# Two alternating layers on one core: weights, squares and normalized rows in one ring of eight places, with later reloads and later block sums

## The chip, the cores and the metric

The kernel runs on 1 core of a Trainium2 chip. The metric is the device time of one execution in microseconds (us). Five engines work side by side, each through its own instructions in program order: TensorE (PE; its weight loads are listed as PEld), VectorE (DVE), ScalarE (ACT), GpSimd (POOL) and SyncE (SP). An instruction waits on semaphores until what it needs is there, and everything behind it on the same engine waits with it. All DMA transfers of this kernel are issued from SP, so a transfer that has to wait holds up every transfer behind it.

## The reference, cut to what matters

```python
def A(q, k, v, shift_k, ssm_k, ssm_D):         # S = 2048 tokens, D = 1024 channels
    k_shift = ...                              # causal convolution with 4 taps, per channel
    kv = k_shift * v
    y = irfft(rfft(kv_pad) * rfft(ssm_k_pad))  # causal convolution over all S tokens, per channel
    return q * (y + kv * ssm_D)

def B(x, w1, b1, w2, b2):                      # F = 3584
    h = x @ w1 + b1
    r = where(h > 0, h, 0)
    return (r * r) @ w2 + b2

x = A_q
x = x + A(layernorm(x), A_k, A_v, A_shift_k, A_ssm_k, A_ssm_D)
x = x + B(layernorm(x), B_w1, B_b1, B_w2, B_b2)
x = x + A(layernorm(x), A_k, A_v, A_shift_k, A_ssm_k, A_ssm_D)
x = x + B(layernorm(x), B_w1, B_b1, B_w2, B_b2)
```

Everything is fp32. The long convolution `y` doesn't depend on x, so it is computed once and serves both layers.

## The kernel before, in words

**Units.** The work runs over 8 units, `ORDER` (line 35): a unit is one layer and one block of 512 tokens (four tiles of 128), and does matrix layer B for it. Unit 0 is block 0 of layer 0, unit 1 block 0 of layer 1, and so on; unit 7 is the last. Where two units follow each other on the same block (0 to 1, 6 to 7), a passage (`chain`) turns one unit's output straight into the next one's input, in halves of two tiles.

**Steps.** A unit is a list of steps (`steps`, lines 680 to 703). A step uses one weight tile of 128 x 512: for the first product (m1) half of a column block of w1, for the second (m2) a row block and half of w2. As fp32 products, each number is split into a high part and the rest, and three matmuls (`mm3`, lines 270 to 273) make one product; a step has 12 matmuls of 512 columns. PE does them in step order.

**The life of a weight tile.** It is loaded raw from HBM on SP (`w_load`, lines 731 and 734), ACT copies its high part into the pair tile `whl` (`w_hi`, line 742), and DVE, in the passages also POOL, subtracts to get the rest (`w_lo`, line 750). Some tiles are also stored to HBM as a split pair (`w_store`, line 757, `wd_m`), and later uses load the pair, ready split, with one DMA (line 740); `from_pair` says which. Unit 0 uses raw tiles nearly alone; from unit 1 on about 70 of 112 tiles are pairs. `whl` has six places; raw tiles `wr` had four.

**How far ahead.** `w_advance` (line 759) runs once at each step s with its weight w: subtractions up to w + 3 (`W_LO`), copies up to w + 4 (`W_HI`), pair loads up to w + 5 (`W_PAIR`), raw loads up to w + 8 (`W_LOAD`) as long as fewer than `RAWS` = 4 raw tiles wait for their subtraction. A raw load thus takes the place that the subtraction of the same step, or one just before it, has to free. A pair load takes the place of the weight six before it, and is issued when that weight's last step lies before s.

**Squares and rows.** After each m1 block `relu2` (line 1102) makes `r` on ACT (relu, square, high part; lines 1105 to 1108) and one step later DVE subtracts (line 1113); `r` had two places of its own. Normalized rows `xn` (lines 631, 1143, 1182), which PE transposes for the next unit, had two as well.

**The convolution.** It is done by blocks of 256 tokens in a transformed domain, alongside units 0 to 5. `fwd_x` and `fwd_g` transform the inputs (ticks of their own; PE transposes and matmuls in the two banks `pt`, DVE and ACT around them) and store the spectra (xd, gd). `prod_stream` (line 439) loads for a group of channels pairs of tiles cx and cg (lines 510 and 512, two places each), multiplies them into `cp` (`mult`, line 445, three places) and sums over the blocks (`red`, line 449). It has a clock of its own, `lag`, that ticks once per product; the product stands two ticks behind its loads, its sum three, and the closing steps (`fin`: combine, split, back transform, scale, store) from tick four on. One product in 14 (`VMOD`) runs on DVE, the others on POOL. How many products go into a step is paced by `pace`, up to two per step in unit 0.

**Within a step** the order of issue is: delayed work that is due (`lag.tick`), `w_advance` (subtractions, copies and pair loads, raw loads), the matmuls, `w_store`, then the convolution's products and transforms.

**The first block.** Block 0's convolution and the first 8 weight tiles are ordered by a planner with costs (`Plan`, line 87; `weight`, line 1036), which also knows how many places `wr` has.

The functions that the change touches, and what calls them:

Of the kernel before, what the change touches and what calls it, by code (L numbers as in the profile page):

```python
# [33 lines left out]
EPS = 1e-5  # L34
ORDER = [(0, 0), (1, 0), (0, 1), (0, 2), (1, 1), (1, 2), (0, 3), (1, 3)]
PAIRS = ((2, 0), (0, 1), (1, 2))
W_LOAD, W_HI, W_LO, W_PAIR = 8, 4, 3, 5
RAWS = 4
PAIR_GAP = 10
PRO_M = "GGV"  # L40
VMOD = 14
FWD_WAIT = 4
PLAN_H = 0.5
VX = 300
# [141 lines left out]
def tile_h3_mlp(ctx: ExitStack, tc: tile.TileContext, q, kT, vT, shk, ssmT, ssmD, w1, b1, w2, b2,  # L186
# [244 lines left out]
        for g in streams:  # L431
            next(g, None)

    count = [0]
    done = set()

    plag = Later()
# [1 line left out]
    def prod_stream():  # L439
        lag = plag  # L440
        sums, inv = [0, 0], [0, 0]

        def mult(st, xt, gt, j, e):
            pr = cv.tile([P, CU, j + 1], F32, name="cp", bufs=3)
            e.tensor_mul(pr.rearrange("p c i -> p i c"), xt[:, 0:j + 1], gt[:, j::-1])  # L445
            st["pr"] = pr

        def red(st, sm, ty, jj):
# [47 lines left out]
        for sb in range(1, NB):  # L496
            nb = BT * sb + BT
            for ch in range(KT):
                while (sb, ch) not in fwd_done:
                    lag.tick()  # L500
                    yield None
                for g in (2 * ch, 2 * ch + 1):
                    while sums[0] - sums[1] >= 2:
                        lag.tick()
                        yield None
                    sums[0] += 1
                    sm = cv.tile([P, 3, BT, CU], F32, name="sm", bufs=2)
                    for ty, (xi, gi) in enumerate(PAIRS):
                        xt = cv.tile([P, nb, CU], F32, name="cx", bufs=2)
                        SY.dma_start(xt, XD[xi][g, :, :nb])  # L510
                        gt = cv.tile([P, nb, CU], F32, name="cg", bufs=2)
                        SY.dma_start(gt, GD[gi][g, :, :nb])
                        for jj in range(BT):
                            j = BT * sb + jj
                            count[0] += 1
                            e = V if count[0] % VMOD == 0 else G
                            st = {}
                            lag.at(2, mult, st, xt, gt, j, e)
                            lag.at(3, red, st, sm, ty, jj)
                            if ty == 2 and jj == BT - 1:  # L520
                                lag.at(4, fin, st, sm, sb, g, 0)
                            lag.tick()
                            yield (j + 1) * CU * 1e-3
        while lag.due:
# [77 lines left out]
    def prep_b(l, b, lag):  # L602
# [4 lines left out]
        def stage(st, tt, k):  # L607
# [7 lines left out]
            elif k == 1:  # L615
                x = st["x"]
                for h in range(2):
                    sl = slice(h * 512, (h + 1) * 512)
                    yt = st["y"][h]
                    V.scalar_tensor_tensor(yt, x[:, sl], mv[:, tt, 0:1], yt, op0=OP.subtract, op1=OP.mult)  # L620
                    V.scalar_tensor_tensor(x[:, sl], yt, r[:, tt:tt + 1], x[:, sl], op0=OP.mult, op1=OP.add)
            elif k == 2:
                st["mv"] = pre.tile([P, 1, 2], F32, name="mv2", bufs=4)
                stats(st["x"], st["mv"][:, 0])
                st["ve"], st["sd"] = rstd_a(st["mv"])
                SY.dma_start(X1[b][:, tt], st["x"])
            elif k == 3:
                st["r"] = rstd_b(st["ve"], st["sd"])
                st["xn"] = []
                for kh in range(2):  # L630
                    xn = ml.tile([P, 512], F32, name="xn", bufs=2)
                    normalize(xn, st["x"][:, kh * 512:(kh + 1) * 512], st["mv"][:, 0, 0:1], st["r"])
                    st["xn"].append(xn)
            elif k == 4:
                st["o"] = []
                for kh in range(2):
                    o = ps1()
                    for c in range(4):
                        PE.transpose(o[:, c * P:(c + 1) * P], st["xn"][kh][:, c * P:(c + 1) * P], ident)  # L639
                    st["o"].append(o.rearrange("p (k t) -> p k t", k=4))  # L640
            else:
# [78 lines left out]
    def from_pair(w):  # L720
        return split_kept(wsrc[w]) and w - first_w[wsrc[w]] >= PAIR_GAP

    def w_load():
        w = ptr["load"]
        ptr["load"] += 1
        if from_pair(w):
            return
        k, c, a, i = wsrc[w]
        raw = raws[w] = mw.tile([P, 512], F32, name="wr", bufs=RAWS)
        if k == "m1":  # L730
            SY.dma_start(raw, w1[c * FC + a, :, 4 * i:4 * i + 4])
        else:
# [3 lines left out]
    def w_hi():  # L736
        n = ptr["hi"]
        t = his[n] = mw.tile([P, 2, 512], F32R, name="whl", bufs=6)
        if from_pair(n):
            SY.dma_start(t.bitcast(F32), WD[wsrc[n]])  # L740
        else:
            A.copy(t[:, 0], raws[n])  # L742
        ptr["hi"] += 1

    def w_lo():
        n = ptr["lo"]
        t = wts[n] = his.pop(n)
        if not from_pair(n):
            e = WLO.get(phase[0], "V")
            ENG[e[n % len(e)]].tensor_sub(t[:, 1], raws.pop(n), t[:, 0].bitcast(F32))  # L750
        ptr["lo"] += 1

    def w_store(w):
# [2 lines left out]
            WD[key] = dram.tile([P, 2, 512], F32, name="wd_" + "_".join(map(str, key)))  # L756
            SY.dma_start(WD[key], wts[w].bitcast(F32))

    def w_advance(s, w, first=False):
        n = len(wsrc)  # L760

        def free(k):
            return k < n and (k < 6 or last_use[k - 6] < s)

        def ahead(k):
            return w + (W_PAIR if k < n and from_pair(k) else W_HI)
# [2 lines left out]
            w_lo()  # L769
        while free(ptr["hi"]) and ptr["hi"] <= ahead(ptr["hi"]) and ptr["hi"] < ptr["load"]:  # L770
            w_hi()
        while ptr["load"] < n and len(raws) < RAWS and ptr["load"] <= w + W_LOAD:
            w_load()
        while ptr["lo"] <= w:
            if ptr["hi"] <= ptr["lo"]:
                w_hi()
            w_lo()
# [4 lines left out]
    def first_block():  # L782
# [305 lines left out]
            wts.pop(w)  # L1088
        for k in ptr:
            ptr[k] = n  # L1090
        return [x.t for x in xT]

    xT = first_block()
# [7 lines left out]

    def relu2(st, k):
        if k == 0:
            r = st["r"] = ml.tile([P, T], F32, name="r", bufs=2)
            A.activation(r, st["o"], AF.Relu, bias=b1t[:, st["f"]:st["f"] + 1])  # L1105
            A.activation(r, r, AF.Square)  # L1106
            st["hi"] = ml.tile([P, T], F32R, name="rh", bufs=FC + 1)
# [2 lines left out]
                give(st["o"])  # L1110
        else:
            st["lo"] = ml.tile([P, T], F32R, name="rl", bufs=FC + 1)
            V.tensor_sub(st["lo"], st["r"], st["hi"].bitcast(F32))  # L1113

    def evict(os, accs, dh):
        d = slice(dh * 512, (dh + 1) * 512)
# [3 lines left out]
    def chain(accs, b, xh, xl, ready):  # L1120
# [13 lines left out]
        def astep(st, n):  # L1134
# [3 lines left out]
                V.scalar_tensor_tensor(x, y, r, x, op0=OP.mult, op1=OP.add)  # L1138
            else:
                for h in range(2):  # L1140
                    z = ml.tile([P, 512], F32, name="xn", bufs=2)
# [3 lines left out]
                    G.tensor_add(x[:, sl], x[:, sl], y[:, sl])  # L1145

        def evict1(st, os, dh):
            d = slice(dh * 512, (dh + 1) * 512)
# [4 lines left out]
        def stage(st, k):  # L1153
# [23 lines left out]
            elif k in (5, 6):  # L1177
# [1 line left out]
                x, m, r = accs[tts[n]], st["mv"][:, n, 0:1], st["r"][:, n:n + 1]  # L1179
                st["o", n] = []  # L1180
                for kh in range(2):
                    xn = ml.tile([P, 512], F32, name="xn", bufs=2)
# [9 lines left out]
            elif k in (7, 8):  # L1192
                n = k - 7
                for kh in range(2):
                    o = ps1()
                    for c in range(4):
                        PE.transpose(o[:, c * P:(c + 1) * P], st["o", n][kh][:, c * P:(c + 1) * P], ident)
                    st["o", n][kh] = o.rearrange("p (k t) -> p k t", k=4)
            else:
                n = k - 9  # L1200
                for kh in range(2):
# [215 lines left out]
```

## Time and profile before

| | us |
|---|---|
| median of 3 runs | 3097.34 (3093.33 to 3100.3) |
| the profiled execution, its time | 3092.24 |
| its span, first to last instruction | 3090.4 |
| PE busy | 2862.2 (93%) |
| DVE busy | 1713.9 (55%) |
| ACT busy | 979.7 (32%) |
| POOL busy | 882.1 (29%) |
| moved by DMA | 704.73 MB, mean 228 GB/s |

All times in the rows below are counted from the first instruction of the profiled execution. In the view by stretches a row gives the stretch, its length, then for each engine the busy time and the number of instructions, the share of full clock that TensorE was granted, the share of the 16 DMA engines that was busy, and GB/s. In the views of waits a row reads: who waited, on which line, for whom; us in total, times, longest. SPq is the queue of SyncE. In the timeline a row gives start, duration, engine, line, operation, tiles and shapes, and in brackets how long the engine stood idle before it and what ended that. The order in which the program issues its work, with the step at which a tile's place was freed, can be counted from the code without any run; where the text counts so, it says "program order".

### The profile page before, as it was taken

How to read it: one execution, taken by the hardware profiler on the slowest of the kernel's cores; microseconds unless marked ns; L12 is line 12 of the kernel's file. 1: busy time of each engine (PE TensorE's matmuls, PEld its weight loads, DVE VectorE, ACT ScalarE, POOL GpSimd, SP SyncE). 2: the span in 40 equal slices, each digit the busy share in tenths (PEclk: the TensorE clock that was granted, in tenths of full speed). 3: DMA queues.
4: the chain of work that ended last, by engine and by line, in shares of the span. 5: the costliest groups of instructions: out<-in, count | busy, mean ns of one | idle time of the engine just before them, and what ended most of it. 6: DMA issues, size and time to landing. Idle time of an engine off the chain costs nothing.

```text
span 3090.4 us, 37259 instructions
## 1 busy us (share of the span) xinstructions
PE 2862.2 (93%) x13512; PEld 2389.9 (77%) x13512; DVE 1713.9 (55%) x2600; ACT 979.7 (32%) x1741; POOL 882.1 (29%) x639
## 2 busy tenths in 40 slices
PE   6877777777999999999999999999999999989999
PEld 6865665656877888888888888888888888878887
DVE  7875545656576777877676664446422621262122
ACT  3332323232333343234323342224222422223222
POOL 5543223334253415542433243331300100030000
PEclk8878888888999999999999999999999999989999
DMA  6445776666787888978887777668654755464543
GB/s 200 132 169 198 233 262 216 224 220 241 255 293 262 274 301 290 324 264 276 288 298 256 249 269 275 228 227 291 216 167 155 265 162 173 143 219 150 185 145 126
DMA packets 332375, 704.73 MB, mean 228 GB/s; under 512 B 55960, under 2 KB 135968, under 8 KB 332192
## 3 DMA queue, kind: packets, MB, share of 16 engines
q1 hardware_dynamic: 332192, 702.36, 67.2%
q8 instruction: 106, 1.74, 0.2%
q14 instruction: 77, 0.63, 0.1%
HBM read 575.36 MB, written 126.88 MB: 227 GB/s over the span
## 4 chain that ended last, share of the span: by engine, by line
PE 66%; DMA 9%; DVE 7%; POOL 2%; SPq 2%; issue 2%; ACT 1%; POOLq 0%; DVEq 0%; ACTq 0%
PE p L271 21%; PE p L273 21%; PE p L272 21%; DMA cg<-gd 4%; POOL cp L445 1%; DVE whl L750 1%; PE pt L272 1%; PE pt L273 1%; PE pt L271 1%; DMA yt<-yd 1%; DMA xd<-fx 1%; DMA wr<-w 1%; DVE sm L449 1%; PE p L639 1%; DMA wd_m<-whl 0%
## 5 line engine op out<-in xcount | busy, mean ns | idle before, releaser
L445 POOL TENSOR_TENSOR cp<-cx,cg 128x384 f32<-128x384 f32 (+5 forms) x268 | 482.8, 1814 | 1128.7 <-DMA cg<-gd 1043.3
L271 PE MATMUL p<-whl,rh 128*128 128x512 f32 x1792 | 722.3, 403 | 20.8 <-DVE acc L1118 16.3
L272 PE MATMUL p<-whl,rh 128*128 128x512 f32 x1792 | 718.8, 401 | 18.9 <-DVE whl L750 13.3
L273 PE MATMUL p<-xh,whl 128*128 128x512 f32 (+1 forms) x1864 | 715.2, 384 | 14.4 <-DVE whl L750 14.3
L271 PE MATMUL p<-xh,whl 128*128 128x512 f32 (+1 forms) x1864 | 718.8, 386 | 6.9 <-ACT r L1105 6.9
L273 PE MATMUL p<-whl,rl 128*128 128x512 f32 x1792 | 716.3, 400 | 0.0
L272 PE MATMUL p<-xl,whl 128*128 128x512 f32 (+1 forms) x1864 | 714.5, 383 | 0.0
L1113 DVE TENSOR_TENSOR rl<-r,rh 128x512 fp32r<-128x512 f32 x224 | 194.8, 870 | 547.8 <-ACT rh L1108 547.6
L750 DVE TENSOR_TENSOR whl<-wr,whl 128x512 fp32r<-128x512 f32 x408 | 349.2, 861 | 157.0 <-ACT whl L742 148.2
L273 PEld LDWEIGHTS p<-xh,whl 128*128 128x128 f32 x1864 | 357.5, 192 | 84.5 <-DVE whl L750 16.7
L742 ACT CAST whl<-wr 128x512 fp32r<-128x512 f32 x419 | 257.1, 618 | 520.4 <-PE p L273 359.7
L271 PEld LDWEIGHTS p<-whl,rh 128*128 128x128 f32 x1792 | 344.5, 192 | 99.7 <-issue 16.4
L272 PEld LDWEIGHTS p<-whl,rh 128*128 128x128 f32 x1792 | 344.2, 192 | 99.9 <-DVE whl L750 16.4
L271 PEld LDWEIGHTS p<-xh,whl 128*128 128x128 f32 x1864 | 358.3, 192 | 72.3 <-ACT r L1105 7.8
L272 PEld LDWEIGHTS p<-xl,whl 128*128 128x128 f32 x1864 | 357.9, 192 | 65.2 <-DVE xl L1032 0.3
L273 PEld LDWEIGHTS p<-whl,rl 128*128 128x128 f32 x1792 | 344.1, 192 | 80.8
L449 DVE TENSOR_REDUCE sm<-cp 128x128 f32<-128x384 f32 (+5 forms) x288 | 251.8, 877 | 247.7 <-POOL cp L445 247.4
L1105 ACT ACTIVATE r<-p,b1t 128x512 f32<-128x512 f32 x221 | 152.1, 688 | 710.3 <-PE p L273 707.2
L1118 DVE TENSOR_TENSOR acc<-p,acc 128x512 f32<-128x512 f32 x240 | 161.5, 688 | 246.6 <-PE p L273 245.7
L1106 ACT ACTIVATE r<-r 128x512 f32<-128x512 f32 x224 | 141.7, 632 | 7.1
L1108 ACT CAST rh<-r 128x512 fp32r<-128x512 f32 x224 | 139.1, 621 | 7.2
L1227 POOL TENSOR_TENSOR acc<-acc,b2t 128x1024 f32<-128x1024 f32 x24 | 64.6, 2719 | 259.8 <-DMA acc<-x 259.8
(201 smaller groups left out, 2774.0 us busy)
## 6 DMA issues: line engine op xcount, KB each, us to landing
whl<-wd_m SPq DMA_DIRECT2D x509, 512.0 KB, 3.7
wr<-w SPq DMA_DIRECT2D x427, 256.0 KB, 4.1
wd_m<-whl SPq DMA_DIRECT2D x70, 512.0 KB, 4.6
cx<-xd SPq DMA_DIRECT2D x48, 512.0 KB, 6.2
cg<-gd SPq DMA_DIRECT2D x48, 512.0 KB, 6.9
gd<-fg SPq DMA_DIRECT2D x72, 256.0 KB, 4.1
cx<-xd SPq DMA_DIRECT2D x48, 384.0 KB, 5.2
cg<-gd SPq DMA_DIRECT2D x48, 384.0 KB, 5.7
```

The lines of the kernel that those rows point to most:

```text
L271: PE.matmul(o, lh, rh, start=start, stop=False)
L272: PE.matmul(o, lh, rl, start=False, stop=False)
L273: PE.matmul(o, ll, rh, start=False, stop=stop)
L445: e.tensor_mul(pr.rearrange("p c i -> p i c"), xt[:, 0:j + 1], gt[:, j::-1])
L449: V.tensor_reduce(sm[:, ty, jj], st["pr"], axis=AX.X, op=OP.add)
L742: A.copy(t[:, 0], raws[n])
L750: ENG[e[n % len(e)]].tensor_sub(t[:, 1], raws.pop(n), t[:, 0].bitcast(F32))
L1105: A.activation(r, st["o"], AF.Relu, bias=b1t[:, st["f"]:st["f"] + 1])
L1106: A.activation(r, r, AF.Square)
L1108: A.copy(st["hi"], r)
L1113: V.tensor_sub(st["lo"], st["r"], st["hi"].bitcast(F32))
L1118: V.tensor_add(accs[tt][:, d], o, accs[tt][:, d])
```

## The change

Raw weight tiles, squares and normalized rows no longer have 4 + 2 + 2 places of their own but share one ring of 8 (`row`, `drop`): each takes the place of the eighth before it, whoever that was. A raw load is issued only if that place was freed before the step ahead of the current one (`room`), so its reader lies at least two steps back. `row` itself, if the place isn't free yet, first issues outstanding copies and subtractions of weights. Pair loads are issued up to w + 4 instead of w + 5, and only if the last step of the weight six before lies two steps back (`free`). All products run on POOL (`VMOD` goes), the sums stand four ticks behind the loads instead of three, and the closing steps follow one tick later too.

```diff
-W_LOAD, W_HI, W_LO, W_PAIR = 8, 4, 3, 5
-RAWS = 4
+W_LOAD, W_HI, W_LO, W_PAIR = 8, 4, 3, 4
+RAWS = 8
 PAIR_GAP = 10
 PRO_M = "GGV"
-VMOD = 14
...
-        def mult(st, xt, gt, j, e):
+        def mult(st, xt, gt, j):
             pr = cv.tile([P, CU, j + 1], F32, name="cp", bufs=3)
-            e.tensor_mul(pr.rearrange("p c i -> p i c"), xt[:, 0:j + 1], gt[:, j::-1])
+            G.tensor_mul(pr.rearrange("p c i -> p i c"), xt[:, 0:j + 1], gt[:, j::-1])
...
-                            count[0] += 1
-                            e = V if count[0] % VMOD == 0 else G
                             st = {}
-                            lag.at(2, mult, st, xt, gt, j, e)
-                            lag.at(3, red, st, sm, ty, jj)
+                            lag.at(2, mult, st, xt, gt, j)
+                            lag.at(4, red, st, sm, ty, jj)
                             if ty == 2 and jj == BT - 1:
-                                lag.at(4, fin, st, sm, sb, g, 0)
+                                lag.at(5, fin, st, sm, sb, g, 0)
...
+    ring, now = [], [0]
+
+    def room():
+        return len(ring) < RAWS or ring[-RAWS].get("freed", now[0]) < now[0] - 1
+
+    def row():
+        while len(ring) >= RAWS and "freed" not in ring[-RAWS]:
+            w_hi() if ptr["lo"] == ptr["hi"] else w_lo()
+        x = {"t": mw.tile([P, 512], F32, name="wr", bufs=RAWS)}
+        ring.append(x)
+        return x
+
+    def drop(*xs):
+        for x in xs:
+            x["freed"] = now[0]
+
     def w_load():
...
-        raw = raws[w] = mw.tile([P, 512], F32, name="wr", bufs=RAWS)
+        raws[w] = row()
+        raw = raws[w]["t"]
...
     def w_lo():
...
-            ENG[e[n % len(e)]].tensor_sub(t[:, 1], raws.pop(n), t[:, 0].bitcast(F32))
+            ENG[e[n % len(e)]].tensor_sub(t[:, 1], raws[n]["t"], t[:, 0].bitcast(F32))
+            drop(raws.pop(n))
...
-    def w_advance(s, w, first=False):
+    def w_advance(s, w):
         n = len(wsrc)
+        now[0] = s
 
         def free(k):
-            return k < n and (k < 6 or last_use[k - 6] < s)
+            if k >= n or k >= 6 and last_use[k - 6] >= s:
+                return False
+            return not from_pair(k) or k < 6 or last_use[k - 6] < s - 1
...
-        while ptr["load"] < n and len(raws) < RAWS and ptr["load"] <= w + W_LOAD:
+        while ptr["load"] < n and ptr["load"] <= w + W_LOAD and (from_pair(ptr["load"]) or room()):
             w_load()
         while ptr["lo"] <= w:
+            if ptr["load"] <= ptr["hi"]:
+                w_load()
             if ptr["hi"] <= ptr["lo"]:
                 w_hi()
             w_lo()
...
     def relu2(st, k):
         if k == 0:
-            r = st["r"] = ml.tile([P, T], F32, name="r", bufs=2)
+            st["r"] = row()
+            r = st["r"]["t"]
...
-            V.tensor_sub(st["lo"], st["r"], st["hi"].bitcast(F32))
+            V.tensor_sub(st["lo"], st["r"]["t"], st["hi"].bitcast(F32))
+            drop(st["r"])
...
-                    xn = ml.tile([P, 512], F32, name="xn", bufs=2)
+                    st["n", n] = [*st.get(("n", n), ()), row()]
+                    xn = st["n", n][-1]["t"]
...
+                drop(*st["n", n])
```

The rows `xn` in `prep_b` and `z` in `astep` change in the same way as the last two parts show.

More of the change, by code (lines that the diff above doesn't have):

```diff
@@ L432, in fwd_tick @@
             next(g, None)
-    count = [0]
     done = set()
@@ L630, in stage @@
                 for kh in range(2):
-                    xn = ml.tile([P, 512], F32, name="xn", bufs=2)
+                    st["n"] = [*st.get("n", ()), row()]
+                    xn = st["n"][-1]["t"]
                     normalize(xn, st["x"][:, kh * 512:(kh + 1) * 512], st["mv"][:, 0, 0:1], st["r"])
@@ L640, in stage @@
                     st["o"].append(o.rearrange("p (k t) -> p k t", k=4))
+                drop(*st["n"])
             else:
@@ L741, in w_hi @@
         else:
-            A.copy(t[:, 0], raws[n])
+            A.copy(t[:, 0], raws[n]["t"])
         ptr["hi"] += 1
@@ L1090, in first_block @@
             ptr[k] = n
+        ring.extend({"freed": 0} for _ in range(n))
         return [x.t for x in xT]
@@ L1140, in astep @@
                 for h in range(2):
-                    z = ml.tile([P, 512], F32, name="xn", bufs=2)
+                    zr = row()
+                    z = zr["t"]
                     sl = slice(h * 512, (h + 1) * 512)
@@ L1145, in astep @@
                     G.tensor_add(x[:, sl], x[:, sl], y[:, sl])
+                    drop(zr)
         def evict1(st, os, dh):
@@ L1181, in stage @@
                 for kh in range(2):
-                    xn = ml.tile([P, 512], F32, name="xn", bufs=2)
+                    st["n", n] = [*st.get(("n", n), ()), row()]
+                    xn = st["n", n][-1]["t"]
                     xs = x[:, kh * 512:(kh + 1) * 512]
```

## The prediction

> **What bounds the kernel now.** I began with the busy time by stretches, cut where the work changes: the first block, unit 0, unit 1 up to where idle stops, the long middle, the late units, the passage from unit 6 to unit 7.
>
> ```profile
> core 0: us, PE busy (x) PEld busy (x) DVE busy (x) ACT busy (x) POOL busy (x), PEclk, DMA share, GB/s
> 0.00:212.00 212.00, 156.50 (x1051) 150.31 (x1052) 162.00 (x298) 67.48 (x138) 106.76 (x120) 0.79 0.50 161
> 212.00:735.00 523.00, 387.33 (x1678) 315.58 (x1677) 302.38 (x469) 162.86 (x305) 174.93 (x153) 0.85 0.70 231
> 735.00:1100.00 365.00, 346.29 (x1745) 293.08 (x1744) 259.79 (x389) 128.98 (x236) 149.71 (x104) 0.96 0.79 263
> 1100.00:2200.00 1100.00, 1098.23 (x5109) 910.23 (x5109) 724.06 (x1005) 377.84 (x666) 408.70 (x240) 1.00 0.78 271
> 2200.00:2700.00 500.00, 500.00 (x2209) 410.73 (x2208) 143.96 (x242) 140.42 (x231) 12.80 (x7) 1.00 0.55 183
> 2700.00:2800.00 100.00, 89.59 (x480) 77.12 (x480) 59.11 (x106) 33.05 (x57) 29.17 (x16) 0.91 0.56 196
> ```
>
> From 1100 to 2700 us PE never rests and has its full clock: whatever the change does there cannot show as a gain. The time to be had lies in unit 0, 212 to 735: there PE does 1678 matmuls in 523 us, while the middle does 5109 in 1100, 0.215 us each, so 1678 would take 361 us (an estimate: the mix of shapes differs a little). That is 162 us lost, in idle time and in the lower clock after it (0.85), though no engine and not the DMA (0.70) is full. So unit 0 is bound by a ring of waits. Next I read who waits there, for PE, for the engines behind it, and for the DMA queue on SP.
>
> ```profile
> PE pt L348 <- DVE fg L408: 38.1, 6, 11.4
> PE p L271 <- DVE acc L1118: 15.6, 2, 7.8
> DVE sm L449 <- POOL cp L445: 165.9, 51, 12.3
> POOL cp L445 <- DMA cg<-gd: 303.7, 36, 35.1
> SPq L734 <- DVE whl L750: 142.1, 36, 12.2
> SPq L731 <- DVE whl L750: 83.7, 24, 9.1
> ```
>
> PE waits for DVE; DVE waits 166 us for products of POOL; POOL waits for its operands cg; and SP, which issues those, stands 226 us (142.1 + 83.7) before a load of raw weights, until DVE has freed one of the four places by its subtraction in line 750. That closes the ring, and the timeline shows one turn of it, by SP, POOL and DVE:
>
> ```profile
> 275.63 0.33 SPq L734 DMA_DIRECT2D wr<-w  x1
> 276.49 0.43 SPq L512 DMA_DIRECT2D cg<-gd  x1
> 289.09 0.33 SPq L734 DMA_DIRECT2D wr<-w  x1
> 290.42 0.94 SPq L512 DMA_DIRECT2D cg<-gd  x1
> 281.35 3.23 POOL L445 TENSOR_TENSOR cp<-cx,cg 128x384 f32<-128x384 f32 x3 [7.66 <-DMA cg<-gd]
> 286.80 1.72 POOL L445 TENSOR_TENSOR cp<-cx,cg 128x512 f32<-128x512 f32 x1
> 295.64 1.02 POOL L445 TENSOR_TENSOR cp<-cx,cg 128x384 f32<-128x384 f32 x1 [7.13 <-DMA cg<-gd]
> 282.40 0.55 DVE L449 TENSOR_REDUCE sm<-cp 128x128 f32<-128x384 f32 x1 [6.79 <-POOL cp L445]
> 287.31 1.75 DVE L750 TENSOR_TENSOR whl<-wr,whl 128x512 fp32r<-128x512 f32 x1
> 290.04 0.68 DVE L303 TENSOR_TENSOR fx<-fx 128x512 f32<-128x512 f32 x1
> ```
>
> cg is issued at 276.49, POOL starts at 281.35 (4.9 us), DVE's sum, the first thing in DVE's order that needs it, starts at 282.40 after 6.79 us idle; line 750, behind it, ends at 289.06; at once SP's raw load goes out (289.09), and behind it the next cg at 290.42. One turn: 13.9 us, and the program gives it only some two and a half steps (the load waits for a subtraction of its own step; the sum stands three ticks behind its operands, at up to two ticks a step). A step at PE's rate would be 361 us / 126 steps = 2.9 us, two and a half of them 7.2.
>
> **The change part by part**
>
> *Eight shared places, loads two steps behind the reader.* No instruction is added. A raw load now goes out only into a place whose reader stood at least two steps earlier; walking the program order, 64 of unit 0's 113 loads take a place freed exactly two steps before, the rest older ones. So SP no longer waits for DVE's work of the same step, and what it drags along, cx and cg above all, goes out two steps earlier against DVE. With the sum one tick later, the same 13.9 us turn spans about five steps, 5 x 2.9 = 14.5 us at PE's full rate: it just stops binding. What is late next? Three candidates, each with a floor for unit 0. PE: 361 us. The two places each of cx and cg: 46 pairs of loads, two pairs per turn of 4.9 us (issue to POOL, above) and four products, two of 1.02 and two of 1.72 us by the rows above, so 23 x 10.4 = 239 us; no bound, though in bursts SP can stand before them. The DMA:
>
> ```profile
> DMA packets 72508, 121.04 MB, mean 231 GB/s; under 512 B 13708, under 2 KB 34188, under 8 KB 72480
> 800.00:900.00 100.00, 95.94 (x451) 79.32 (x450) 74.53 (x108) 30.84 (x58) 38.86 (x29) 0.97 0.88 294
> 1200.00:1300.00 100.00, 100.00 (x488) 83.82 (x487) 77.77 (x113) 27.10 (x51) 44.72 (x32) 1.00 0.93 318
> ```
>
> Unit 0 moves 121.04 MB (the DMA view of 212:735). Sustained over 100 us the case shows 294 GB/s with PE nearly full and 318 at the most: 412 or 381 us. I take 412: unit 0 goes from 523 to 412, **-111 us**. Bounds: 381 (-142), and from the other side 121.04 MB at 263 GB/s, the mean of 735:1100, which is 460 (-63).
>
> *Unit 1 and the passages.* There most weights come ready split, and SP waits for PE:
>
> ```profile
> SPq L740 <- PE p L273: 1413.5, 457, 9.3
> whl<-wd_m SPq DMA_DIRECT2D x509, 512.0 KB, 3.7
> PE p L272 <- DVE whl L750: 5.1, 2, 4.9
> DVE xn L1187 <- PE p L1197: 2.1, 1, 2.1
> ```
>
> The pair load of 4 instead of 5 ahead takes the same place, free at the same end of PE's work; only SP comes to it a step later in its own order, so what stands behind it goes out up to one step (2.9 us) sooner. From the place's release to its use lie five steps, 14 us, against 3.7 us to landing. In the middle this is worth 0, its cover being that slack; were it gone, every us late would be a us for PE. In 735:1100 PE idles 365 - 346.3 = 18.7 us, part of it behind DVE's line 750 (5.1 us of it): I take **-8** (bounds 0 and -18.7). In 2700:2800 PE idles 10.4 us; normalized rows had two places and DVE waited 2.1 us there for PE's transposes, which eight places end: **-2** (0 to -10).
>
> *Squares in the ring.* A new wait: in unit 0, 20 of 28 squares rows take a place that DVE freed only one step before, so ACT's relu (and behind it the raw copies and PE's second product) can now stand behind line 750. No row shows that wait. Nearest rows:
>
> ```profile
> PE p L271 <- ACT r L1105: 6.9, 2, 5.9
> L750 DVE TENSOR_TENSOR whl<-wr,whl x408: 672/684/2904, 214.9 to 3068.3; 128x512 fp32r<-128x512 f32 x136
> ```
>
> Below: 0, if DVE is no more than a step behind. Above: 20 x 5.9 us, the longest stall that a late relu gave PE, 118 us. I take 20 x 0.4, a little over half of one subtraction: **+8**; the lower end is nearer, since the sums that made DVE late now stand a tick further off.
>
> *All products on POOL, sums a tick later.*
>
> ```profile
> L445 POOL TENSOR_TENSOR cp<-cx,cg x268: 988/1855/3116, 268.8 to 2192.5; 128x384 f32<-128x384 f32 x27, 128x896 f32<-128x896 f32 x25, 128x768 f32<-128x768 f32 x23, 128x640 f32<-128x640 f32 x22
> L445 DVE TENSOR_TENSOR cp<-cx,cg x20: 1055/1610/2823, 336.4 to 2143.4; 128x768 f32<-128x768 f32 x7, 128x1024 f32<-128x1024 f32 x7, 128x512 f32<-128x512 f32 x6
> ```
>
> 20 products of 1.61 us leave DVE (32 us of its 1714), 20 of 1.86 us (37 us) join POOL, busy 29%: 0, since both engines have idle time beside PE; it covers about 45% of DVE. If DVE set the pace it would be worth up to -32; lost through POOL no more than +37. The sums and the closing steps a tick later move no block over its deadline: in the program order the last closing step of each sequence block stays in the same step. 0.
>
> The Trainium skill (SBUF — State Buffer, section "Who interferes with whom") speaks against this part: a DVE instruction with two SBUF inputs and a POOL instruction that reads SBUF exclude each other for the whole instruction. The trace agrees: beside POOL's product at 286.80 line 750 took 1.75 us, without one line 303 of the same shape 0.68. By that rule each of the 20 could hold DVE up some 1.1 us, 21 of the 32 us given back.
>
> *The first block.* Eight places let the planner order all of it anew, the four later weight loads sooner. Its PE idles 212 - 156.5 = 55.5 us now; I see no reason for a sign: 0, bounds +-10 (an estimate, a fifth of that idle time).
>
> Sum: -111 - 8 - 2 + 8 = -113. The profiled execution took 3092.2 us (span 3090.4), so 2979; the median shown, 3097.3, is 5.1 above it: **2984 us**.
>
> **The rivals**
>
> *Little gain (15%).* The ring is not all: ACT and POOL wait for DVE in other places (69.2 us of ACT before the copies in line 400), PE holds the transform banks meanwhile, and unit 0 only gets its DMA share from 0.70 to 0.75: 523 x 0.70 / 0.75 = 488, -35, about 3062. For it: such waits remain. Against: the DVE they wait for is late because of the sums.
>
> ```profile
> ACT fg L400 <- DVE pt L393: 69.2, 8, 14.8
> 380.00:400.00 20.00, 20.00 (x95) 16.58 (x94) 7.07 (x12) 10.34 (x19) 0.43 (x1) 1.00 1.02 351
> ```
>
> *More gain (12%).* DMA isn't the next bound: in 380:400 PE is full while the DMA moves 351 GB/s, at which unit 0 would take 345 us, less than PE's 361. Then -162, all 18.7 of unit 1 and 2: 3097.3 - 183 = 2914. Against: no stretch of 100 us shows that rate.
>
> *Slower (6%).* Squares on ACT behind DVE's subtractions: a wait takes the place of the one removed. If DVE stays more than one step (2.9 us) late, all 20 rows stall and, at 5.9 us each for PE, add 118 us while the old ring goes on through ACT and gives no gain: 3215. With the gain kept it decides from 111 / 20 = 5.6 us a row on.
>
> *It doesn't do what it says (5%).* The ring itself throttles: 64 loads still wait for DVE, and those of two steps before are as late as those of one. Then 3097, no change.
>
> **How the numbers follow.** The forecast has 62%, its own range 2943 to 3042: the DMA's 381 us (31 below the 412) and 460 (48 above), each with the first block's 10. The whole range leaves out the large gain (12%) and the slower case (6%) and takes in the small gain: 2930 to 3062. Within 0.2% is what a measurement of this kernel can't tell from no change. Faster: forecast, little and more gain, 89%, less a little for unknown costs: 0.88. Same 0.05, slower 0.07.
>
> **What would show it.** Right: in unit 0 SP's waits for line 750 fall from 226 us to under 60, DVE's for POOL from 166 to under 60, PE's clock there goes above 0.93, the DMA share to 0.85 or more; the middle stays at 1.00. Wrong: ACT's relu waiting for DVE in line 750's place; PE waiting for pairs (whl from wd_m) after 1100; unit 0 still above 480 us.

## The result, and the profile after

| | before | after |
|---|---|---|
| median of 4 runs, us | 3097.24 (3093.33 to 3100.3) | 2971.98 (2968.6 to 2974.17) |
| ratio, 95% interval | | 0.9595 (0.9579 to 0.9612) |
| the profiled execution, its time | 3092.24 | 2974.17 |
| its span | 3090.4 | 2972.4 |
| first block (to the first relu on ACT) | 211.9 | 215.6 |
| unit 0 (to the first transposes of the first passage) | 522.5 | 423.0 |
| rest of the first passage and unit 1 (to the first transposes for unit 2) | 351.6 | 336.1 |
| middle (to the first transposes of the last passage) | 1663.8 | 1659.8 |
| last passage and unit 7 | 340.6 | 337.9 |

The kernel became 4.0% faster. Of the 118 us between the two profiled executions, 99.5 came out of unit 0. This is the busy time of the kernel after by those stretches (columns as before):

```profile
core 0: us, PE busy (x) PEld busy (x) DVE busy (x) ACT busy (x) POOL busy (x), PEclk, DMA share, GB/s
0.00:215.60 215.60, 164.18 (x1050) 157.00 (x1051) 161.50 (x296) 67.32 (x138) 111.06 (x122) 0.78 0.52 173
215.60:638.60 423.00, 363.06 (x1676) 298.25 (x1674) 311.74 (x462) 160.62 (x304) 190.59 (x159) 0.93 0.84 278
638.60:974.70 336.10, 327.27 (x1688) 279.41 (x1689) 246.11 (x362) 121.40 (x222) 148.58 (x103) 0.98 0.81 274
974.70:2634.50 1659.80, 1655.76 (x7571) 1368.48 (x7569) 901.94 (x1312) 538.44 (x935) 466.37 (x267) 1.00 0.71 244
2634.50:2972.40 337.90, 326.09 (x1532) 271.63 (x1532) 94.07 (x150) 88.19 (x144) 19.81 (x10) 0.98 0.46 155
```

In unit 0 PE still has the same 1676 matmuls. Its granted clock rose from 0.85 to 0.93, and the DMA, with almost the same bytes, from 231 to 278 GB/s: less standing, not less work. Who still waits there is in the waits of unit 0, 215.6 to 638.6 (all eight-place tiles are now called wr, so line 1128 is the relu; line 443 is the product, 447 its sum, 746 and 749 the raw loads, 765 the subtraction of weights, 1136 that of squares):

```profile
POOL cp L443 <- DMA cg<-gd: 162.5, 24, 29.0
DVE sm L447 <- POOL cp L443: 60.7, 14, 11.1
ACT fg L399 <- DVE pt L392: 56.6, 8, 11.2
...
PE pt L347 <- DVE fg L407: 18.3, 5, 6.0
PE pt L270 <- DVE fx L312: 12.8, 4, 6.0
...
SPq L508 <- POOL cp L443: 68.1, 28, 5.5
...
SPq L746 <- DVE whl L765: 19.1, 10, 3.1
...
SPq L746 <- DVE rl L1136: 11.4, 1, 11.4
...
SPq L749 <- DVE whl L765: 3.5, 8, 1.2
SPq L749 <- DVE rl L1136: 3.4, 5, 1.5
```

SP's wait for the weights' subtraction, 226 us before, is 22.6 (19.1 + 3.5). Since squares now share the places, a raw load can also wait for their subtraction (line 1136), 14.8 us: together 37.4. DVE's for POOL's products fell from 166 to 60.7, POOL's for cg from 304 to 162.5, PE's for the transform bank (now line 347) from 38.1 to 18.3. SP has a new place where it stands longest, before the loads of cx, whose two places POOL frees: 68.1 us.

### The profile page after: what moved, and what is told of

Read it like the earlier page. It is cut to its first block, busy times and chain, and to the rows that moved or that the text cites. A ratio compares the mean times of both kernels' runs of the same rounds, so it can differ in the third digit from the quotient of the medians.

```text
span 2972.4 us, 37140 instructions
## 1 busy us (share of the span) xinstructions
PE 2836.3 (95%) x13512; PEld 2374.8 (80%) x13512; DVE 1715.4 (58%) x2578; ACT 976.0 (33%) x1741; POOL 936.4 (32%) x661
## 4 chain that ended last, share of the span: by engine, by line
PE 77%; DVE 11%; DMA 6%; issue 2%; POOL 1%; ACT 1%; SPq 1%; DVEq 0%; POOLq 0%; ACTq 0%
PE p L270 24%; PE p L271 24%; PE p L272 24%; DMA cg<-gd 2%; DVE whl L765 2%; PE pt L271 2%; PE pt L272 1%; PE pt L270 1%; DMA xd<-fx 1%; DVE sm L447 1%; DMA wd_m<-whl 1%; DMA wr<-w 1%; POOL cp L443 1%; DVE rl L1136 1%; PE p L636 1%
## 5 line engine op out<-in xcount | busy, mean ns | idle before, releaser
L443 POOL TENSOR_TENSOR cp<-cx,cg 128x384 f32<-128x384 f32 (+5 forms) x288 | 531.0, 1859 | 917.3 <-DMA cg<-gd 662.6
L1136 DVE TENSOR_TENSOR rl<-wr,rh 128x512 fp32r<-128x512 f32 x224 | 208.5, 931 | 560.1 <-ACT rh L1131 559.4
L765 DVE TENSOR_TENSOR whl<-wr,whl 128x512 fp32r<-128x512 f32 x408 | 361.8, 892 | 175.5 <-ACT whl L757 174.4
L1128 ACT ACTIVATE wr<-p,b1t 128x512 f32<-128x512 f32 x221 | 152.5, 690 | 718.7 <-PE p L272 714.8
L1129 ACT ACTIVATE wr<-wr 128x512 f32<-128x512 f32 x224 | 141.7, 633 | 7.1
L1131 ACT CAST rh<-wr 128x512 fp32r<-128x512 f32 x224 | 139.1, 621 | 7.1
```

The costliest lines, as they stand in the source:

```text
L443: G.tensor_mul(pr.rearrange("p c i -> p i c"), xt[:, 0:j + 1], gt[:, j::-1])
L765: ENG[e[n % len(e)]].tensor_sub(t[:, 1], raws[n]["t"], t[:, 0].bitcast(F32))
L1131: A.copy(st["hi"], r)
L1136: V.tensor_sub(st["lo"], st["r"]["t"], st["hi"].bitcast(F32))
```

## Experiments

Times are medians of four runs; stretches and waits come from each kernel's profiled execution. "Ratio" is to the kernel before on the same chip, with its 95% interval. None of these kernels leaves out or alters a computation.

**One part of the change undone.** Four kernels start from the kernel after. The sums go back to tick three:

```diff
-                            lag.at(4, red, st, sm, ty, jj)
+                            lag.at(3, red, st, sm, ty, jj)
...
-                                lag.at(5, fin, st, sm, sb, g, 0)
+                                lag.at(4, fin, st, sm, sb, g, 0)
```

> The changed kernel, with the block sums back at three ticks behind their loads (closing steps from tick four), all else kept. Theory of the ring of waits (SP's raw load behind DVE's subtraction, cg behind the raw load, POOL behind cg, DVE's sum behind POOL, the subtraction behind the sum): the two steps of room still stretch the turn of some 13.9 us over about four and a half steps, 13 us at 2.9 us a step, so it binds only a little: unit 0 grows from 423 us by 5 to 25, in all 2977 to 2997 us. Rival, that the gain came from DVE no longer meeting an unfinished product: most of the 100 us of unit 0 goes back, 3040 to 3075 us. In both, DVE's waits for products in unit 0 rise above the 60.7 us of the changed kernel.

Measured: 2989.11, ratio 0.965 (0.9623 to 0.9677), 17 us slower than the change, inside the theory's range; unit 0 took 431.1 (8.1 more) and DVE waited there longer for POOL than the 60.7 us of after:

```profile
DVE sm L447 <- POOL cp L443: 84.6, 28, 10.6
```

The sum's tick is worth 17 us on top of the rest. Next, a load may take a place as soon as it is freed, in the same step too:

```diff
-        return len(ring) < RAWS or ring[-RAWS].get("freed", now[0]) < now[0] - 1
+        return len(ring) < RAWS or "freed" in ring[-RAWS]
```

> The changed kernel, in which a raw load may take a place as soon as it is freed in the program order, thus also in the same step; eight shared places, sums at four ticks and the rest kept. Theory of the ring of waits: SP again stands before DVE's subtraction of its own step, the turn of 13.9 us spans about three steps, 4.5 us each: unit 0 at 480 to 510 us, in all 3030 to 3060, SP's waits for the subtractions in unit 0 back above 120 us. Rival, that the sums a tick later made the gain: within 15 us of the changed kernel, 2957 to 2987. Rival, that four more places are the gain, however early they are taken: the same 2957 to 2987, with SP's waits under 60 us.

Measured: 2974.36, ratio 0.9606 (0.9579 to 0.9633), unit 0 in 422.3. My theory, that the rule of two steps breaks the ring, missed by 56 us or more. SP did stand longer before raw loads, in unit 0 (218.2 to 640.5) for 73.3 us (43.5 + 15.9 + 13.9) where the kernel after has 37.4, with no loss clear of the intervals. It stood less elsewhere: all its waits in unit 0, added up over the rows of the view, are 215 us here and 221 in the kernel after.

```profile
SPq L508 <- POOL cp L443: 57.2, 26, 4.7
SPq L749 <- DVE rl L1136: 43.5, 14, 7.0
...
SPq L746 <- DVE whl L765: 15.9, 12, 3.2
SPq L746 <- DVE rl L1136: 13.9, 2, 9.6
```

The program order says why so little changed: loads go no further than eight weights ahead, so with eight places only 17 of unit 0's 117 raw loads (the 113 of the prediction and the first four) meet a place freed in the same step, and 16 one step before. The rule kept only these apart from what they would have been without it; what it was to test stayed open, and so did which of the two rivals holds. The last experiment of this section takes it up.

One product in 14 goes back to DVE:

```diff
+VMOD = 14
...
+                            count[0] += 1
+                            e = V if count[0] % VMOD == 0 else G
```

> The changed kernel, with one product in 14 on DVE again (20 products of 1.6 us), all else kept. Theory: both engines have idle time, 0 to +6 us, 2966 to 2982. Rival, that DVE sets the pace in unit 0 by its own work: +15 to +32 us, the whole of the 32 us that leave DVE, 2987 to 3004.

Measured: 2973.04, ratio 0.9601 (0.9568 to 0.9634): nothing, as expected. The pair loads go back to five ahead without the margin:

```diff
-W_LOAD, W_HI, W_LO, W_PAIR = 8, 4, 3, 4
+W_LOAD, W_HI, W_LO, W_PAIR = 8, 4, 3, 5
...
-            return not from_pair(k) or k < 6 or last_use[k - 6] < s - 1
+            return True
```

> The changed kernel, with the pair loads up to five ahead and issued at the step right behind the old reader's last, as before; the ring of eight, room and sums kept. Theory: unit 0, which has 7 pair loads, stays at 423 us; what stands behind the pair loads on SP goes out a step later from unit 1 on, which gives back part of the 15.5 us that the stretch from the first passage to the next unit's transposes gained: 2977 to 2990 us. Rival, that this gain came from the ring and the sums as well: 2968 to 2976.

Measured: 2980.18, ratio 0.9621 (0.9593 to 0.965), in which the change's 0.9595 lies. Where the profiled execution lost is told by its stretches: unit 1 kept its time (336.7), the middle went from 1659.8 to 1666.3. The middle of this kernel, split at 2000 and 2600 us:

```profile
974.50:2000.00 1025.50, 1021.11 (x4758) 846.30 (x4757) 676.23 (x957) 356.11 (x630) 397.63 (x232) 1.00 0.79 272
2000.00:2600.00 600.00, 600.00 (x2660) 493.11 (x2659) 204.24 (x312) 174.80 (x289) 55.09 (x29) 1.00 0.57 193
```

The same of the kernel after:

```profile
974.90:2000.00 1025.10, 1024.98 (x4791) 851.42 (x4790) 679.04 (x971) 356.02 (x632) 401.81 (x232) 1.00 0.79 274
2000.00:2600.00 600.00, 599.61 (x2653) 492.92 (x2652) 199.55 (x297) 174.94 (x289) 54.51 (x29) 1.00 0.57 192
```

PE idles 4.4 us (1025.5 less 1021.11) where the kernel after idles 0.1, and has done 33 matmuls fewer by 2000 us, 7 us at 0.215 each. So the later pair load earns a little in the middle, not in unit 1 where I had put it; the intervals overlap, so its size is not sure.

**One part alone.** From the kernel before, the sums at tick four, and nothing else:

```diff
-                            lag.at(3, red, st, sm, ty, jj)
+                            lag.at(4, red, st, sm, ty, jj)
...
-                                lag.at(4, fin, st, sm, sb, g, 0)
+                                lag.at(5, fin, st, sm, sb, g, 0)
```

> The kernel before, with its block sums four ticks behind the loads and the closing steps from tick five, nothing else. Theory, as the first four runs leave it (the load that takes a place of its own step is what closes the ring of waits; a tick more in the sums only stretches it): 20 to 40 us of gain, 3055 to 3075, with SP's waits for subtractions in unit 0 still above 120 us. Rival, that the sums made most of the gain and the ring little: 2985 to 3010.

Measured: 3054.32 against 3093.87 before, ratio 0.9864 (0.9844 to 0.9883): 40 us, a little more than the range. Unit 0 took 491.7, at a clock of 0.87. Then everything but the ring: sums at tick four, all products on POOL, the later pair loads, four places for raw weights as before (the sums' lines, and these):

```diff
-W_LOAD, W_HI, W_LO, W_PAIR = 8, 4, 3, 5
+W_LOAD, W_HI, W_LO, W_PAIR = 8, 4, 3, 4
...
-                            e = V if count[0] % VMOD == 0 else G
+                            e = G
...
-            return k < n and (k < 6 or last_use[k - 6] < s)
+            if k >= n or k >= 6 and last_use[k - 6] >= s:
+                return False
+            return not from_pair(k) or k < 6 or last_use[k - 6] < s - 1
```

> The kernel before with all of the change but the ring of eight: four raw places and two each for squares and normalized rows, sums at four ticks, all products on POOL, pair loads four ahead and two steps behind the reader. Theory: like the kernel before with the later sums alone, less up to 8 us for the pair loads: 3045 to 3070 us; unit 0 at 480 to 505 us. Rival, that the parts beside the ring make the gain together: under 3000.

Measured: 3031.16, ratio 0.9792 (0.9773 to 0.981); the range was missed by 14 us, on the good side. Unit 0 took 480.6. So the ring of eight is worth 59 us of the whole (3031.2 less 2972.0), 57.6 of them in unit 0.

This kernel is 23 us under the one with the sums alone, where up to 8 were expected. The products on POOL and the later pair loads were not tried apart here, so which of them it was stays open. The kernel with the sums alone shows one wait that the products take with them when they leave DVE: in unit 0 (215.2 to 706.9) DVE stood before its own products until cg had landed.

```profile
DVE cp L445 <- DMA cg<-gd: 10.2, 4, 5.8
```

**Bytes.** The kernel after, with every split pair stored a second time to another tensor (70 transfers of 512 KB, 67 of them in unit 0):

```diff
+    WX = [dram.tile([P, 2, 512], F32, name="wx")]
...
             SY.dma_start(WD[key], wts[w].bitcast(F32))
+            SY.dma_start(WX[0], wts[w].bitcast(F32))
```

> The changed kernel, in which each of the 70 split pairs is stored a second time, to a tensor that nobody reads: 35 MB more, all but a few of them in unit 0. If the DMA is what unit 0 is bound by now (0.84 of its time, 278 GB/s), its 423 us grow by 35 MB / 294 GB/s, 119 us, in all about 3090 us. If it is still the waits between engines, with the DMA only busy beside them: 20 to 60 us, 2992 to 3032.

Measured: 3023.39, ratio 0.9772 (0.9749 to 0.9795). Unit 0 grew by 47.5 us to 470.5, where the bytes alone would have cost some 119 if the DMA, at 294 GB/s, were the bound. Its row, and the longest wait of SP there:

```profile
216.20:686.70 470.50, 376.60 (x1676) 306.79 (x1675) 309.78 (x462) 161.36 (x304) 188.35 (x159) 0.88 0.93 327
```
```profile
SPq L775 <- DMA wx<-whl: 68.7, 35, 5.7
```

The DMA carried 327 GB/s for 470 us. At that rate the bytes of unit 0 in the kernel after (278 GB/s x 423.0 us = 117.6 MB) would need 360 us (an estimate). It is the rate of another mix, though: the added stores bring some 10000 packets to the 71420 of unit 0, and only 1100 of them are under 2 KB, where 34064 of the others are. The busy share allows for that: unit 0 of the kernel after takes 0.84 x 423.0 = 355 us of all 16 engines, which at the share of 0.93 reached here would fit into 382 us (an estimate too). Either way the DMA's rate does not set its 423.

**What sets unit 0 now.** The kernel after, with at most four raw tiles waiting, so that loads go out some seven weights ahead, as before the change, into still older places:

```diff
-        while ptr["load"] < n and ptr["load"] <= w + W_LOAD and (from_pair(ptr["load"]) or room()):
+        while ptr["load"] < n and ptr["load"] <= w + W_LOAD and (from_pair(ptr["load"]) or len(raws) < 4 and room()):
```

> The changed kernel, in which besides at most four raw tiles may wait for their subtraction, as before: the raw loads then run seven steps ahead as they did before (86 of 117 in unit 0), but into places freed two steps or more before. It tells apart what eight places give. Theory, that it is the place's age (no wait on SP for DVE's work of the same step): within 10 us of the changed kernel, 2965 to 2985, SP's waits for subtractions in unit 0 under 60 us. Rival, that it is the earlier load itself, which reaches ACT before it is needed: half or more of the gain goes, above 3030.

Measured: 2965.08, ratio 0.958 (0.9562 to 0.9598). Loading earlier is not what the eight places give: with the loads as late as before, the gain stays, and in the profiled execution unit 0 is 9 us shorter still (the intervals of the whole overlap):

```profile
215.30:629.20 413.90, 358.48 (x1677) 295.05 (x1675) 309.86 (x462) 160.77 (x304) 194.90 (x159) 0.93 0.84 284
```

Then the wait before cx: while the first sequence block of the stream is convolved (`sb == 1`, the one that unit 0 works on, whose tiles fill half a place), each place takes two pairs of tiles.

```diff
-                        xt = cv.tile([P, nb, CU], F32, name="cx", bufs=2)
+                        if sb == 1:
+                            if half[0] % 2 == 0:
+                                both = [cv.tile([P, 2 * nb, CU], F32, name=n_, bufs=2) for n_ in ("cx", "cg")]
+                            xt, gt = (t_[:, half[0] % 2 * nb:half[0] % 2 * nb + nb] for t_ in both)
+                            half[0] += 1
+                        else:
+                            xt = cv.tile([P, nb, CU], F32, name="cx", bufs=2)
+                            gt = cv.tile([P, nb, CU], F32, name="cg", bufs=2)
                         SY.dma_start(xt, XD[xi][g, :, :nb])
-                        gt = cv.tile([P, nb, CU], F32, name="cg", bufs=2)
```

> The changed kernel, in which each place of cx and cg holds two pairs of loads while the first sequence block is convolved (its tiles fill half a place), so four pairs are in flight in unit 0 instead of two. SP stands 68 us in unit 0 of the changed kernel before cx until POOL has read the old one. Theory that this is the ring of waits that binds now: SP's wait there falls under 20 us and unit 0 from 423 to 395 to 410 us, in all 2944 to 2960. Rival, that SP only stands there instead of elsewhere and DVE's lateness for PE's transform banks binds: within 6 us of the changed kernel, 2966 to 2978.

Measured: 2967.47, ratio 0.9578 (0.9564 to 0.9593), unit 0 in 416.1. SP's wait before cx for POOL fell from 68.1 to 2.0 us in unit 0 (214.0 to 630.1), and others grew in its place (line 413 stores the filters' spectra, 753 is a raw load; they were 31.4 and 19.1):

```profile
SPq L413 <- DVE fg L407: 39.9, 8, 10.3
SPq L753 <- DVE whl L772: 28.2, 10, 6.4
```

All of SP's waits in unit 0 added up fell from 221 to 215 us only: the 68 us were mostly waiting that SP would have done elsewhere. Both edits together:

> Both together: at most four raw tiles waiting (7 us less than the changed kernel by itself) and two pairs to a place. If the two act on the same queue of SP one after the other, they add: 2935 to 2955 us. If the earlier raw loads only hurt because SP was crowded, four raws gain nothing more here: as the run with two pairs to a place alone, within 4 us.

Measured: 2966.07, ratio 0.9576 (0.956 to 0.9592), unit 0 in 415.1: they don't add. Next, both, with the first block's planner told of four places for weights instead of eight:

```diff
-                raw = new(mw, "wr", RAWS, [P, 512])
+                raw = pl.buf("wr", 4, lambda: mw.tile([P, 512], F32, name="wr", bufs=RAWS))
```

> As the run before, and the planner of the first block is told of four raw places again (the order of the first block then stays that of the kernel before; its weight tiles rotate through the eight). The first block took 211.9 us in the kernel before and 213 to 218 with eight places in the plan: 2 to 6 us less than the run before.

Measured: 2963.35, ratio 0.9566 (0.955 to 0.9582), the lowest median of all, 8.6 us under the change. But the first block took 215.9, where the run before had 215.8, not less, so the reason given for it fell, and its lead over the two kernels before it lies within their intervals.

**Age of the place or number of places.** The kernel with everything but the ring, four places, but at most three raw tiles waiting: each load goes out later, into a place freed one subtraction earlier. In program order 103 of unit 0's 117 raw loads took a place freed in the same step without this edit; with it, 104 take one freed one step before.

```diff
-        while ptr["load"] < n and len(raws) < RAWS and ptr["load"] <= w + W_LOAD:
+        while ptr["load"] < n and len(raws) < 3 and ptr["load"] <= w + W_LOAD:
```

> The kernel before with the block sums a tick later, all products on POOL and the later pair loads (the one that came to 3031), still with four places of their own for raw weights, but at most three raw tiles waiting instead of four: each load goes out a step later, six weights ahead instead of seven, into a place whose subtraction stood one step earlier instead of in the same step. Theory (the age of the place sets the turn of the ring, not the number of places nor how early the load is issued): SP's waits for line 750 in unit 0 fall from 184 us to under 90, unit 0 from 481 to 425-455 us, the whole to 2975-3005. Rival (it takes the eight places, so that loads have their lead): no gain or a loss, 3025-3050, with waits of PE, ACT or DVE for raw tiles (wr from w) in unit 0.

Measured: 2981.11, ratio 0.963 (0.9606 to 0.9654). The kernel it starts from had this row for unit 0, and these waits of SP:

```profile
210.50:691.10 480.60, 382.96 (x1677) 312.12 (x1676) 302.07 (x462) 162.56 (x304) 185.32 (x159) 0.86 0.75 251
```
```profile
SPq L734 <- DVE whl L750: 109.1, 33, 9.5
SPq L731 <- DVE whl L750: 74.4, 28, 8.3
```

With three raw tiles waiting:

```profile
214.00:644.00 430.00, 366.65 (x1676) 300.24 (x1674) 307.98 (x462) 162.38 (x304) 189.94 (x159) 0.91 0.83 278
```
```profile
SPq L734 <- DVE whl L750: 68.2, 30, 8.0
SPq L731 <- DVE whl L750: 38.5, 17, 6.4
```

One constant gave 50 of the ring's 59 us, with four places and with later loads. SP's wait is still 106.7 us, more than the 90 expected. That fits a ring in which a wait of SP costs only while what stands behind it is what DVE waits for next; no run shows this by itself.

The waits are those of unit 0. SP's are the waits of raw loads for DVE's subtraction of weights, and, where they share places with squares, in brackets those for either subtraction.

| kernel | unit 0 | clock there | SP waits for the weights' subtraction | DVE waits for products | median |
|---|---|---|---|---|---|
| before | 522.5 | 0.85 | 225.8 | 165.9 | 3097.2 |
| sums at tick four | 491.7 | 0.87 | 198.1 | 110.0 | 3054.3 |
| all but the ring | 480.6 | 0.86 | 183.5 | 115.1 | 3031.2 |
| the same, three raws waiting | 430.0 | 0.91 | 106.7 | 71.4 | 2981.1 |
| after | 423.0 | 0.93 | 22.6 (37.4) | 60.7 | 2972.0 |
| after, four raws waiting | 413.9 | 0.93 | 8.5 (25.4) | 58.8 | 2965.1 |

## Why the prediction was right, and where its steps were not

The forecast of 2984 lies 12 us above the median. Five of them are the sum's (-113 between the profiled executions, where it was -118); the others come from the profiled execution before, 5 us under its median, and that of after, 2 us over. The lower end of the whole range, 2930, comes from no sum of the prediction; the forecast's own starts at 2943.

*The ring of waits* held. It said that unit 0 is bound by a turn from SP's raw load over cg, POOL and DVE's sum back to the subtraction, and that stretching it frees some 100 us (-111 and +8 for the squares). Unit 0 gave -99.5. Of the marks set for it, SP's wait came under 60 us (22.6, or 37.4 with the squares' subtraction) and the middle kept its clock; DVE's wait for POOL (60.7 against 60), the clock (0.93) and the DMA share (0.84 against 0.85) stopped at the mark or just short of it. The lengths were less sure than they looked. The turn of 13.9 us was read off one turn: in the same timeline the next cg after 290.42 went out at 295.06, 4.6 us later. That five steps of 2.9 us, 14.5 us, just cover it is therefore no proof of the size.

*What stretches the turn* was told too narrowly. The prediction leaned on places freed exactly two steps before. One subtraction of distance already gives most of it (three raws waiting: -50 us of the ring's 59), and a two-step rule on top of eight places does nothing measurable. It also counted the sum's tick into one turn without a price of its own; alone it is worth 40 us, and still 17 when taken out of the change. The parts are not additive, as one expects of edits that loosen the same ring.

*The floor of 412 us* had the right size for the wrong reason. It was worked out as 121 MB at 294 GB/s. With 36 MB more, unit 0 ran at 327 GB/s, and without them it stopped at 423 (414 in the best case) at 278 to 284: that 412 came so near to 423 is luck. What does hold it there isn't settled: PE's largest waits that are left are those for the transform bank (18.3 and 12.8 us above), and no run took those away alone.

*Squares in the ring, +8*: about nothing is seen of it, though no run took the squares out of the ring. The relu waited once for DVE in unit 0:

```profile
ACT wr L1128 <- DVE whl L765: 1.6, 1, 1.6
```

The wait that squares did bring is one that the prediction had not listed: SP's raw loads behind their subtraction, the 14.8 us above.

*Unit 1, -8*: it was -15.5, and not from SP's order. The sums alone brought that stretch from 351.6 to 340.7, all but the ring to 337.3; the pair loads undone left it at 336.7. The term was mostly put down to the wrong edit: PE's largest waits there were for a late DVE, and most of the gain came with the sums. The prediction counted 5.1 us of PE's idle time behind line 750, where its own view of that stretch has 11.0 (5.9 + 5.1). Before, in 734.4 to 1086:

```profile
PE p L273 <- DVE whl L750: 5.9, 1, 5.9
PE p L272 <- DVE whl L750: 5.1, 2, 4.9
PE pt L348 <- DVE fg L408: 3.9, 1, 3.9
```

After, in 638.6 to 974.9:

```profile
PE p L272 <- DVE whl L765: 4.7, 1, 4.7
```

*The middle, 0, and the last passage, -2*: -4.0 and -2.7. The pair loads were costed at nothing in the middle with 14 us of slack as cover; undoing them lost some 7 us there in one profile. What was late there, the pair or a transfer behind it in SP's order, was not followed.

*Products on POOL, 0*: right on top of the rest of the change, where taking it back cost nothing (2973.0 against 2972.0). Without the ring of eight it stays open, as said above, since there this part and the pair loads made 23 us together. The sum has a slip too: 1.61 us is the median of the 20 products on DVE; their mean is 1.72, so 34 us left DVE and not 32. The page of after, the busy time of all engines and DVE's two kinds of subtraction:

```profile
PE 2836.3 (95%) x13512; PEld 2374.8 (80%) x13512; DVE 1715.4 (58%) x2578; ACT 976.0 (33%) x1741; POOL 936.4 (32%) x661
...
L1136 DVE TENSOR_TENSOR rl<-wr,rh 128x512 fp32r<-128x512 f32 x224 | 208.5, 931 | 560.1 <-ACT rh L1131 559.4
L765 DVE TENSOR_TENSOR whl<-wr,whl 128x512 fp32r<-128x512 f32 x408 | 361.8, 892 | 175.5 <-ACT whl L757 174.4
```

And the page of the kernel with one product in 14 back on DVE:

```profile
PE 2836.3 (95%) x13512; PEld 2375.3 (80%) x13512; DVE 1723.1 (58%) x2598; ACT 976.1 (33%) x1741; POOL 909.6 (31%) x641
...
L1140 DVE TENSOR_TENSOR rl<-wr,rh 128x512 fp32r<-128x512 f32 x224 | 208.3, 930 | 549.9 <-ACT rh L1135 549.8
L769 DVE TENSOR_TENSOR whl<-wr,whl 128x512 fp32r<-128x512 f32 x408 | 346.5, 854 | 178.2 <-ACT whl L761 170.6
```

These two kernels differ in the 20 products alone, which took 33.5 us on DVE in the second. DVE's busy time differs by 7.7 us only; the subtraction of weights is 15.3 us longer without them, that of squares the same. So some of the 33.5 are given back, but one pair of profiles doesn't tell how much: over the kernels here that have all products on POOL, DVE's busy time ranges from 1700.0 to 1717.6 us, which is 5.5 to 23.1 below 1723.1, so 10 to 28 are given back. The rule of the Trainium skill (SBUF — State Buffer, "Who interferes with whom"), by which a DVE instruction with two SBUF inputs and a POOL instruction that reads SBUF exclude each other, made it 21 of 32: that lies in this range, which is too wide to confirm it.

*The first block, 0 within 10*: +3.7 in the profile, while it ranged from 210.5 to 218.2 over all these kernels.

## What to carry to other kernels

Where one in-order queue issues both refills and the operands of another engine, look at how long ago the place of each refill was freed, before asking for more places: with four places and one tile fewer in flight 50 of the 59 us that the eight places gave were there. Price each edit that loosens the same ring of waits alone and on top of the rest; the two differ (40 and 17 us here). A wait at one place of a queue is no loss by itself: 36 us more before raw loads cost nothing that could be measured in one of these kernels, and 66 us less before cx brought 4.5 us in another, within the intervals; the queue's waits as a whole (221, 215 and 215 us in unit 0) hardly changed.

## What was unexpected of the hardware

The DMA of one core carried 327 GB/s over 470 us, once 67 stores of 512 KB more stood in unit 0; in the kernel before, 294 to 318 over 100 us had been the most beside a busy PE. And 20 products that took 33.5 us on DVE shortened its busy time by 5 to 23 us only when they moved to POOL, while in the one pair of profiles that differs in them alone DVE's subtraction of weights became longer (854 to 892 ns each).
